# Expert inputs: nine gathers of quarter tokens replaced by three gathers of whole tokens, a store in slot order and four plain loads

## The chip, the core and the metric

The kernel runs as one program on one core of one Trainium2 chip. The metric is device time in microseconds (us), lower is better; the number quoted is the median of several runs, and one more execution was recorded by the hardware profiler. Where this text says PE, DVE, ACT, POOL and SP it means the engines TensorE, VectorE, ScalarE, GpSimd and SyncE.

## What is computed

Local plus pooled attention gives 2304 tokens of 512 numbers. Two mixture-of-experts layers follow. In the first, each token goes to one of 8 experts, and each expert takes exactly 288 tokens:

```python
order = np.argsort(-flat)                 # gate logits of all (token, expert) pairs
for idx in order:
    tok, e = (int(idx) // E, int(idx) % E)
    if assigned[tok] >= 0 or counts[e] >= cap:
        continue
    assigned[tok] = e
...
for e in range(E):
    mask = assigned == e
    h = np.maximum(x[mask] @ w1[e], 0.0)
    out[mask] = h @ w2[e]
```

The second layer is a soft mixture: 32 slots are weighted sums over all tokens, each slot passes through an expert's two layers, and each token takes a weighted sum of the slots.

## The kernel before, in words

**Stages.** Attention writes the tokens to device memory as `x_dram`, one row of 2 KB for each token (L261). The gating stage finds the assignment by bisection (rounds) and `dispatch` turns it into a table of token numbers: `idx` is 96 x 24, and column 3e + c holds the tokens of slots 96c to 96c + 95 of expert e. At the end of `gating` stands a branch (`tc.If`, L876) on a flag: a slow exact path that these inputs don't take. All engines pass that branch before the expert stage begins; the text calls the moment at which they go on the join.

**Expert stage.** `moe` (L1155) runs a loop over e from -2 to 8. Each round issues the steps of a list written out by hand (`START` for e up to 0, `PERIOD` for 1 to 6, `END` for 7 and 8), and that list alone fixes the order on each engine; engines wait for each other through semaphores. A step ("gather", 1) in round e works for expert e + 1. The steps that matter here:

- `gather(e)`, L1178: brings the 288 tokens of expert e into the tile `xs`, cut in quarters: partition 32a + t of block b holds quarter a (128 numbers, 512 B) of token 32b + t. That takes nine indirect DMAs on POOL's queue, each with 128 row numbers out of `idx4`, a table of 128 x 72 that `dispatch` works out from `idx` with three matmuls and three DVE operations (L808 to L817). Expert 0 is different: its tokens come by `first_gather` (L1147, three indirect DMAs of 96 whole tokens, still before the branch) and are transposed on PE (L1195).
- `x_t(e, dt)`, L1185: for e over 0, four times a 32 x 32 block transpose of `xs` on DVE (L1202), then the split in a high part on ACT (L1203) and a low part on DVE (L1204). The next expert's gather may write `xs` only when all four transposes of this one are done.
- `split` (weights in a high and a low part, L1209 and L1211), `hidden` (twelve matmuls for each of eight column blocks, L1224 to L1227), `relu`, `h_rows`, `logits2`, `soft`, `weighted` (18 matmuls, L1310), `slots` (L1323), `scatter` (three indirect DMAs on POOL, L1302).

**Weights.** `Stream` loads them on SP's queue in tiles of 1 MB. A load is issued when a slot comes free, in the order of the list `todo`, and SP waits in order: what stands behind a waiting load waits too. Slots are 8 tiles `a` (they hold second-layer weights of experts 4 to 7 until those are used), 9 tiles `b`, and near the end `xs`, `x0`, `x1`, `P`, `c0`.

## Time and profile before

| what | value |
|---|---|
| median of 3 runs | 460.2 us (459.11 to 460.39) |
| the profiled execution, its own time | 457.83 us |
| its span (first to last instruction) | 455.7 us |
| PE busy | 399.2 us, 88% of the span |
| DVE, ACT, POOL busy | 280.0, 204.3, 172.3 us |
| bytes moved by DMA | 111.54 MB, mean 245 GB/s |
| the gathers L1180 on POOL | 63 instructions, 66.7 us busy |

The busy share of an engine says little here, since the stages have different limits: the expert stage runs from 216 to 406 us, and what a change in it is worth is read from the waits of PE there. Times in rows are counted from the start of the span. The 2.1 us between the span and the execution's own time lie around the program.

### The profile page before, as it was taken

To read this page: it belongs to the slowest core of one execution; us is meant where nothing else is said; L and a number is where in the kernel's file an instruction comes from. 1 tells how busy PE (TensorE), PEld (TensorE's weight loads), DVE (VectorE), ACT (ScalarE), POOL (GpSimd) and SP (SyncE) were. 2 spreads that over 40 slices of the span, in tenths; PEclk is the share of its full clock that TensorE was granted. 3 is DMA by queue.
4 is the path that set the end of the run, shared out by engine and by line. 5 is a ranking of instruction groups with operands and counts; after the bars stand their busy time and mean duration, and the time that the engine had idled before them with its cause. 6 is when DMAs were issued, how large, how long until landed. Compare 5 with 4: busy or idle time off the path is not lost.

```text
span 455.7 us, 11232 instructions
## 1 busy us (share of the span) xinstructions
PE 399.2 (88%) x4386; PEld 297.8 (65%) x4386; DVE 280.0 (61%) x741; ACT 204.3 (45%) x554; POOL 172.3 (38%) x274
## 2 busy tenths in 40 slices
PE   5897988988979779995969999999999999579994
PEld 5675656655545547763868797979797977343694
DVE  6667849667583647873456676675867673414263
ACT  0555343353433427883445555645555554302241
POOL 7254353352343310002717474747466402212000
PEclk9799989999998798999699999999999999899997
DMA  8878999999999739901133566676748497959995
GB/s 218 211 212 227 275 250 296 280 239 306 257 265 272 305 94 399 424 22 55 44 109 134 199 236 229 235 259 217 263 168 311 131 378 285 420 192 355 410 378 233
DMA packets 33210, 111.54 MB, mean 245 GB/s; under 512 B 7328, under 2 KB 16928, under 8 KB 24352
## 3 DMA queue, kind: packets, MB, share of 16 engines
q1 hardware_dynamic: 28000, 100.43, 64.8%
q10 hardware_dynamic: 2176, 5.31, 5.0%
q0 software_dynamic: 2976, 5.02, 3.9%
q8 instruction: 37, 0.61, 0.5%
q14 instruction: 21, 0.17, 0.1%
HBM read 101.01 MB, written 9.73 MB: 243 GB/s over the span
## 4 chain that ended last, share of the span: by engine, by line
PE 27%; DVE 7%; ACT 6%; POOL 5%; issue 4%; DMA 3%; DVEq 0%; ACTq 0%; POOLq 0%
POOL xs L1180 5%; PE g L1310 4%; PE h L1421 3%; DMA xs<-x_dram,idx 3%; ACT bd L1295 3%; PE g L1323 2%; PE h L1224 2%; PE m L1443 2%; PE l L1443 2%; PE h L1225 2%; PE h L1227 2%; PE m L1257 2%; PE t L1224 1%; DVE xs L1202 1%; DVE wl L1211 1%
## 5 line engine op out<-in xcount | busy, mean ns | idle before, releaser
L1180 POOL DMA_INDIRECT xs<-x_dram,idx x63 | 66.7, 1059 | 53.6 <-DVE xs L1202 36.4
L1211 DVE TENSOR_TENSOR wl<-b,wh 128x512 fp32r<-128x512 f32 x64 | 42.9, 681 | 15.5 <-ACT wh L1209 14.9
L1209 ACT ACTIVATE wh<-b 128x512 fp32r<-128x512 f32 x64 | 39.1, 623 | 11.7 <-PE h L1225 6.8
L1224 PE MATMUL h<-x,wh 128*128 128x288 f32 x128 | 39.3, 328 | 4.2 <-ACT wh L1209 4.2
L1310 PE MATMUL g<-hb,bd 128*128 128x256 f32 x144 | 34.6, 396 | 6.8 <-ACT bd L1295 6.8
L1224 PE MATMUL t<-x,wh 128*128 128x288 f32 x128 | 36.7, 309 | 0.7 <-ACT wh L1209 0.7
L1302 POOL DMA_INDIRECT lg_rows<-lt,idx x24 | 22.3, 929 | 37.3 <-DVE lt L1284 30.6
L1225 PE MATMUL h<-x,wh 128*128 128x288 f32 x128 | 36.2, 304 | 0.0
L1310 PEld LDWEIGHTS g<-hb,bd 128*128 128x128 f32 x144 | 27.7, 197 | 12.5 <-ACT bd L1295 8.4
L1225 PE MATMUL t<-x,wh 128*128 128x288 f32 x128 | 35.1, 295 | 0.0
L1224 PEld LDWEIGHTS h<-x,wh 128*128 128x128 f32 x128 | 25.1, 196 | 13.4 <-ACT wh L1209 9.8
L144 POOL TENSOR_TENSOR e<-e,sm 128x256 f32<-128x256 f32 (+1 forms) x24 | 14.6, 608 | 46.9 <-DVE sm L143 35.9
L1242 DVE STREAM_TRANSPOSE hb<-hT 128x288 f32<-128x288 f32 x64 | 27.3, 456 | 0.1
L133 ACT ACTIVATE e<-sd,mx 128x144 f32<-128x144 f32 (+1 forms) x48 | 17.6, 371 | 19.0 <-DVE mx L124 18.0
L1203 ACT ACTIVATE x<-xs 128x288 fp32r<-128x288 f32 x28 | 12.4, 443 | 29.6 <-DVE xs L1202 29.4
L1224 PEld LDWEIGHTS t<-x,wh 128*128 128x128 f32 x128 | 24.1, 188 | 2.3 <-ACT wh L1209 1.7
L1225 PEld LDWEIGHTS h<-x,wh 128*128 128x128 f32 x128 | 25.2, 197 | 0.3
L1225 PEld LDWEIGHTS t<-x,wh 128*128 128x128 f32 x128 | 24.1, 188 | 0.2
L201 ACT ACTIVATE sc<-sc 128x228 f32<-128x228 f32 x24 | 9.3, 393 | 32.3 <-DVE sc L197 32.3
L91 DVE TENSOR_REDUCE kd<-kT 128x288 f32<-128x1152 f32 x16 | 21.5, 1346 | 3.6 <-DMA kT<-in_k_dram 3.6
L1204 DVE TENSOR_TENSOR x<-xs,x 128x288 fp32r<-128x288 f32 x28 | 12.8, 459 | 16.7 <-ACT x L1203 16.7
L1227 PE MATMUL h<-x,wl 128*128 128x288 f32 x128 | 22.7, 301 | 0.0
(289 smaller groups left out, 1014.1 us busy)
## 6 DMA issues: line engine op xcount, KB each, us to landing
b<-in_moe_w_dram SPq DMA_DIRECT2D x35, 1024.0 KB, 7.7
a<-in_moe_w_dram SPq DMA_DIRECT2D x16, 1024.0 KB, 10.4
a<-in_moe_w2t_dram SPq DMA_DIRECT2D x8, 1024.0 KB, 11.3
qT<-in_q_dram SPq DMA_DIRECT2D x8, 576.0 KB, 6.6
x_dram<-xu SPq DMA_DIRECT2D x8, 576.0 KB, 3.4
vn<-in_v_dram SPq DMA_DIRECT2D x8, 512.0 KB, 8.9
b<-in_moe_w_dram SPq DMA_DIRECT2D x7, 512.0 KB, 10.6
a<-in_moe_w_dram SPq DMA_DIRECT2D x6, 512.0 KB, 10.1
```

What stands on the lines that cost most here:

```text
L91: nc.vector.tensor_reduce(s["kd"][:, :, bi], s["kT"][:, :, bi, 3:3 + S].rearrange("p h (t r) -> p h t r", r=4), axis=AX.X, op=ALU.add)
L133: nc.scalar.activation(e[:n, h], p[:n, h], AF.Exp, bias=mx[:n, h:h + 1], scale=1.0 / 128, accum_out=sm[:n, h:h + 1])
L1180: nc.gpsimd.indirect_dma_start(out=xs[:, 128 * b:128 * b + 128], out_offset=None, in_=x_dram.rearrange("n (a d) -> (n a) d", a=4), in_offs ...
L1209: nc.scalar.activation(wh, w, AF.Copy)
L1211: nc.vector.tensor_sub(wl, w, wh.bitcast(F32))
L1224: nc.tensor.matmul(p, wh[:, dt], xh[:, dt], start=dt == 0, stop=False)
L1225: nc.tensor.matmul(p, wh[:, dt], xl[:, dt], start=False, stop=False)
L1227: nc.tensor.matmul(p, wl[:, dt], xh[:, dt], start=False, stop=dt == 3)
L1242: nc.vector.transpose(st["hb", e][:, :, ft], st.pop(("hr", e, ft)).rearrange("p (b t) -> p b t", t=32))
L1302: nc.gpsimd.indirect_dma_start(out=lg_rows[3 * e + c], out_offset=bass.IndirectOffsetOnAxis(ap=idx[:, 3 * e + c:3 * e + c + 1], axis=0), i ...
L1310: nc.tensor.matmul(p, bd[:, b].rearrange("t g s -> t (g s)"), hb[:, b].rearrange("t f r -> t (f r)"), start=b == 0, stop=b == NC - 1)
L1443: nc.tensor.matmul(p[32 * g:32 * g + 32], h2T[gp][:, ft, 32 * g:32 * g + 32], WS["a2", 4 * gp + g, h][:, ft], start=ft == 0, stop=ft == 7, ...
```

## The change

The table `idx4`, its constant `quarter` and the operations that made it are gone. For each expert from 1 on, three indirect DMAs of 96 whole tokens (2 KB each) bring the tokens into a new tile `xg`; one plain DMA on SP stores them as 288 consecutive rows of a new buffer `x_sorted` in device memory; four plain DMAs on SP, one for each quarter and 32 partitions each, load them from there into `xs` in the same layout as before, in pieces of 512 B. The work is spread: `gather(e)` loads expert e, stores e + 1 and gathers e + 2 (the first rounds fill this line). `xg` takes the room of the ninth `b` slot, and becomes a weight slot itself when the last expert has been stored.

```diff
-def gating(nc, tc, ctx, L, C, Z, idx, idx4, fill, first, force=None):
+def gating(nc, tc, ctx, L, C, Z, idx, fill, first, force=None):
...
             verdict(bad, what)
-
-        t96 = sb.tile([96, 24], F32, name="dt96", bufs=1)
-        nc.vector.tensor_copy(t96, idx)
         if what is not None:
             fill.run(psum, "t")
-        i4 = idx4.rearrange("p (c b) -> p c b", b=3)
-        for b in range(3):
-            sl = slice(32 * b, 32 * b + 32)
-            p = psum([128, 24])
-            nc.tensor.matmul(p, C["gsum"][sl], t96[sl], start=True, stop=True)
-            nc.vector.tensor_scalar(i4[:, :, b], p, 4.0, C["quarter"], op0=ALU.mult, op1=ALU.add)
...
     def gather(e):
-        for b in range(NC if e else 0):
+        if e == 0:
+            gather_rows(1)
+            return store_rows(1)
+
+        for a in range(4):
+            nc.sync.dma_start(xs[32 * a:32 * a + 32, 0:128 * NC].rearrange("p (b d) -> p b d", d=128),
+                              x_sorted[CAP * e:CAP * e + CAP, 128 * a:128 * a + 128].rearrange("(b t) d -> t b d", t=32))
+        if e == 1:
+            gather_rows(2)
+        if e + 1 < E:
+            store_rows(e + 1)
+        if e + 2 < E:
+            gather_rows(e + 2)
+        if e + 1 == E - 1:
+            WS.add_slots(mp, ["xg"])
+
+    def gather_rows(e):
+        st["xg"] = mp.tile([128, 2048], F32, name="xg", bufs=1)
+        for c in range(3):
             nc.gpsimd.indirect_dma_start(
-                out=xs[:, 128 * b:128 * b + 128], out_offset=None,
-                in_=x_dram.rearrange("n (a d) -> (n a) d", a=4),
-                in_offset=bass.IndirectOffsetOnAxis(ap=idx4[:, NC * e + b:NC * e + b + 1], axis=0))
+                out=st["xg"][0:96, DM * c:DM * c + DM], out_offset=None, in_=x_dram,
+                in_offset=bass.IndirectOffsetOnAxis(ap=idx[:, 3 * e + c:3 * e + c + 1], axis=0))
+
+    def store_rows(e):
+
+        nc.sync.dma_start(x_sorted[CAP * e:CAP * e + CAP].rearrange("(c w) d -> w c d", w=96),
+                          st["xg"][0:96, 0:3 * DM].rearrange("w (c d) -> w c d", c=3))
...
-        WS.add_slots(wb, [f"b{i}" for i in range(9)])
+        WS.add_slots(wb, [f"b{i}" for i in range(8)])
```

**POOL after the join.** The rows of POOL's program from the start of the expert stage on, before (`bd` is a tile of zeros, `lt` the rows that `scatter` writes; "x9" counts equal instructions):

```order
L1236 MEMSET bd_4095 128x1152
L1180 DMA xs_2606<-x_dram_72,idx4_2609 128x128 x18
L1302 DMA lg_rows<-lt_4404,idx_2608 2304x32 x3
L1180 DMA xs_2606<-x_dram_72,idx4_2609 128x128 x9
L1302 DMA lg_rows<-lt_4650,idx_2608 2304x32 x3
```

and of the change:

```order
L1246 MEMSET bd_4066 128x1152
L1186 DMA xg_4076<-x_dram_71,idx_2604 96x512 x3
L1186 DMA xg_4168<-x_dram_71,idx_2604 96x512 x3
L1186 DMA xg_4173<-x_dram_71,idx_2604 96x512 x3
L1186 DMA xg_4378<-x_dram_71,idx_2604 96x512 x3
L1312 DMA lg_rows<-lt_4384,idx_2604 2304x32 x3
```

Nine indirect DMAs for an expert become three, and before the first `scatter` the change gathers experts 1 to 4 where the kernel before gathered 1 and 2.

**SP after the join.** Before, SP's queue holds weight loads alone there:

```order
L919 DMA b1_4229<-in_moe_w2_dram 128x2048
L919 DMA b0_4284<-in_moe_w1_dram 128x2048
L919 DMA b2_4430<-in_moe_w1_dram 128x2048
L919 DMA b3_4501<-in_moe_w2_dram 128x2048
L919 DMA b4_4553<-in_moe_w2_dram 128x2048
L919 DMA b5_4559<-in_moe_w1_dram 128x2048
```

and of the change:

```order
L1192 DMA x_sorted_72<-xg_4076 96x3x512
L1172 DMA xs_2602<-x_sorted_72 32x9x128 x4
L1192 DMA x_sorted_72<-xg_4168 96x3x512
L907 DMA b1_4209<-in_moe_w2_dram 128x2048
L907 DMA b0_4264<-in_moe_w2_dram 128x2048
L1172 DMA xs_2602<-x_sorted_72 32x9x128 x4
L1192 DMA x_sorted_72<-xg_4173 96x3x512
L907 DMA b2_4410<-in_moe_w1_dram 128x2048
L907 DMA b3_4481<-in_moe_w1_dram 128x2048
L907 DMA b4_4533<-in_moe_w2_dram 128x2048
L907 DMA b5_4539<-in_moe_w2_dram 128x2048
```

In each period four loads and a store of tokens now stand in front of the four weight loads, and with one slot fewer the weight loads run one tile behind: the pair after the first store is both halves of expert 1's second layer, where before one of these was loaded ahead of the branch.

**PE ahead of the branch.** Before (L738 is the matmul of the flag, L530 and L514 are filler work for another tile, L816 makes `idx4`):

```order
L738 MATMUL g_3343<-bad,ones 1x2
L530 MATMUL t<-pt,gsum_70 32x128 x4
L816 MATMUL t<-dt_3347,gsum_70 128x24 x3
L514 MATMUL t<-wT,phi 32x256 x8
L530 MATMUL t<-pt,gsum_70 32x128 x4
L745 TENSOR_LOAD flag
L876 COMPARE_AND_BRANCH
```

and of the change:

```order
L735 MATMUL g_3336<-bad,ones 1x2
L529 MATMUL t<-pt,gsum_70 32x128 x4
L513 MATMUL t<-wT,phi 32x256 x8
L529 MATMUL t<-pt,gsum_70 32x128 x4
L742 TENSOR_LOAD flag
L864 COMPARE_AND_BRANCH
```

The three matmuls for `idx4` are gone from between the two pieces of filler work; nothing else moved on PE there.

## Rows read from the trace of the kernel before

**Rows 1.** Windows of the first expert and a later period: busy, PE clock, DMA share, GB/s.

```profile
212.00:234.00 22.00, 13.52 (x84) 12.88 (x77) 7.88 (x15) 6.78 (x14) 10.34 (x10) 0.77 0.13 39
254.00:275.00 21.00, 20.78 (x149) 17.53 (x150) 14.81 (x34) 11.86 (x29) 12.32 (x12) 1.00 0.66 231
```

**Rows 2.** Timeline of PE, the first matmuls of `weighted` in three periods: start, length.

```profile
295.68 1.56 PE L1310 MATMUL g<-hb,bd 128*128 128x256 f32 x6 [0.23 <-ACT bd L1295]
...
316.61 1.56 PE L1310 MATMUL g<-hb,bd 128*128 128x256 f32 x6 [0.22 <-ACT bd L1295]
...
338.00 1.35 PE L1310 MATMUL g<-hb,bd 128*128 128x256 f32 x5 [0.22 <-ACT bd L1295]
```

**Rows 3.** Timeline of DVE, first transpose for expert 1, 5 and 6; idle before in brackets.

```profile
231.14 0.48 DVE L1202 STREAM_TRANSPOSE xs<-xs 128x288 f32<-128x288 f32 x1 [2.94 <-DMA xs<-x_dram,idx]
...
317.08 0.48 DVE L1202 STREAM_TRANSPOSE xs<-xs 128x288 f32<-128x288 f32 x1 [2.36 <-issue]
...
337.71 0.48 DVE L1202 STREAM_TRANSPOSE xs<-xs 128x288 f32<-128x288 f32 x1 [1.60 <-DMA xs<-x_dram,idx]
```

**Rows 4.** Timeline of PE: its wait in the first expert, idle before in brackets.

```profile
233.48 0.40 PE L1224 MATMUL h<-x,wh 128*128 128x288 f32 x1 [3.14 <-ACT wh L1209]
```

**Rows 5.** Timeline of POOL after the join: first, second and last row of this stretch.

```profile
216.38 1.06 POOL L1236 MEMSET bd<- 128x1152 f32 x1 [4.92 <-DVEq L876]
217.59 0.97 POOL L1180 DMA_INDIRECT xs<-x_dram,idx  x1 [0.15 <-issue]
...
228.36 0.94 POOL L1180 DMA_INDIRECT xs<-x_dram,idx  x1 [0.30 <-issue]
```

**Rows 6.** Line L1150 (first_gather, three times 96 whole tokens): issue to landing.

```profile
DMA to landing us min/median/max: 3.0/3.0/3.0
```

**Rows 7.** Timeline of PE ahead of the branch.

```profile
209.67 0.53 PE L816 MATMUL t<-dt,gsum 32*128 32x24 f32 x6 [0.40 <-DVE dt L809]
210.13 1.07 PE L514 MATMUL t<-wT,phi 128*32 128x256 f32 x16
211.71 0.43 PE L530 MATMUL t<-pt,gsum 128*32 128x128 f32 x8 [0.51 <-ACT pt L518]
```

**Rows 8.** Timeline of ACT ahead of the branch.

```profile
207.69 2.06 ACT L501 ACTIVATE wT<-t 128x512 f32<-128x512 f32 x4 [1.06 <-PE t L499]
```

**Rows 9.** Line L876, the branch on PE's queue: duration in ns, start.

```profile
L876 PEldq COMPARE_BRANCH  x1: 3412/3412/3412, 212.3 to 212.3; - x1
```

**Rows 10.** DMA issues of the page: count, KB each, median us to landing.

```profile
b<-in_moe_w_dram SPq DMA_DIRECT2D x35, 1024.0 KB, 7.7
...
x_dram<-xu SPq DMA_DIRECT2D x8, 576.0 KB, 3.4
...
out_dram<-b SPq DMA_DIRECT2D x4, 576.0 KB, 3.0
```

**Rows 11.** Timeline of SP: a load of V (292.5 KB) into 32 partitions.

```profile
32.89 0.33 SPq L80 DMA_DIRECT2D V<-in_v_around_dram  x1
```

**Rows 12.** Window just behind that load: columns as in rows 1.

```profile
33.50:34.00 0.50, 0.50 (x7) 0.00 (x0) 0.50 (x2) 0.01 (x1) 0.00 (x0) 1.00 0.97 185
```

**Rows 13.** Timeline of SP: two weight loads at the end of a period.

```profile
302.98 1.19 SPq L919 DMA_DIRECT2D b<-in_moe_w_dram  x2
```

**Rows 14.** Windows behind those two loads.

```profile
309.00:310.00 1.00, 1.00 (x8) 0.89 (x7) 0.00 (x0) 0.39 (x2) 0.72 (x1) 1.00 1.08 438
...
311.00:312.00 1.00, 1.00 (x10) 1.00 (x10) 0.87 (x3) 0.97 (x4) 0.73 (x1) 1.00 0.21 66
```

**Rows 15.** Timeline of PE: its wait for the last expert.

```profile
396.31 1.22 PE L1310 MATMUL g<-hb,bd 128*128 128x256 f32 x2 [4.97 <-ACT bd L1295]
```

**Rows 16.** Windows in which the granted PE clock fell (first two) and rose (last).

```profile
214.50:215.00 0.50, 0.00 (x0) 0.00 (x0) 0.00 (x0) 0.00 (x0) 0.00 (x0) 0.91 0.00 0
...
395.50:396.00 0.50, 0.00 (x0) 0.00 (x0) 0.00 (x0) 0.49 (x2) 0.50 (x1) 0.81 0.97 410
399.00:399.50 0.50, 0.50 (x3) 0.44 (x2) 0.00 (x0) 0.00 (x0) 0.00 (x0) 0.77 0.28 79
```

More of the change, by code (lines that the diff above doesn't have):

```diff
@@ L460, in constants @@
     C["gsum"] = pool.tile([128, 128], F32, name="gsum4")
-    C["quarter"] = pool.tile([128, 1], F32, name="quarter")
     return C
@@ L598, in gate_consts @@
     C["pcol"] = pc
-    for g in range(4):
-        nc.gpsimd.memset(C["quarter"][32 * g:32 * g + 32], float(g))
     j = pool.tile([128, NT], F32, name="jrow")
@@ L1152, in first_gather, with moe @@
             in_offset=bass.IndirectOffsetOnAxis(ap=idx[:, c:c + 1], axis=0))
-def moe(nc, tc, ctx, C, WS, P, idx, idx4, mp, xs, x_dram, lg_dram, out):
+def moe(nc, tc, ctx, C, WS, P, idx, mp, xs, x_dram, x_sorted, lg_dram, out):
     ident, gsum = C["ident"], C["gsum"]
@@ L1509, in fused @@
     x_dram = dr.tile([N, DM], F32, name="x_dram")
+    x_sorted = dr.tile([N, DM], F32, name="x_sorted")
     lg_dram = nc.dram_tensor("lg_rows", [N, SL], F32, kind="Internal").ap()
@@ L1550, in fused @@
     idx = mp.tile([96, 24], I32, name="idx")
-    idx4 = mp.tile([128, 9 * E], I32, name="idx4")
     with ExitStack() as gctx:
-        WS.add_slots(wb, [f"b{i}" for i in range(9)])
+        WS.add_slots(wb, [f"b{i}" for i in range(8)])
         for e in range(4, E):
             PM.add(e)
-        gating(nc, tc, gctx, L, C, Z, idx, idx4, PM,
+        gating(nc, tc, gctx, L, C, Z, idx, PM,
                lambda: first_gather(nc, xs, x_dram, idx))
     pctx.close()
-    moe(nc, tc, ctx, C, WS, P, idx, idx4, mp, xs, x_dram, lg_dram, out)
+    moe(nc, tc, ctx, C, WS, P, idx, mp, xs, x_dram, x_sorted, lg_dram, out)
 _INS = ['q', 'k', 'v', 'v_rest', 'v_around', 'moe_w_gate', 'moe_w1', 'moe_w2', 'moe_w2t', 'moe2_phi', 'moe2_w1', 'moe2_w2']
```

## The prediction

> **What bounds the kernel now.** I read the windows by stage first, then the waits of PE, then what ended each. In a period of the expert stage PE is busy 20.78 of 21 us at full clock [rows 1], and the first matmuls of `weighted` follow each other after 20.93 us (295.68 to 316.61) and then 21.39 us (316.61 to 338.00) [rows 2]. So the periods are bound by PE, all but one: in the period with 21.39 DVE stood idle 2.36 us before the first transpose of the next tokens, which began at 317.08, 0.47 after `weighted` had begun [rows 2, 3]. In the neighbour DVE stood idle too (1.60 us), but its transpose at 337.71 came 0.29 ahead of `weighted`, and that period was not longer [rows 2, 3]. The reader is to see that a late gather is free until it pushes the transposes past `weighted`; the excess of 21.39 over 20.92 is then 0.47 us. The chain of waits runs through the gathers in every period all the same, since there they end just in time; a place on that chain is not a saving.
>
> The first expert is another case: in 212 to 234 PE is busy 13.52 of 22 us [rows 1]. All engines go on after the branch at 216.38 [rows 5]. Nine gathers for expert 1 start between 217.59 and 228.36 [rows 5], 1.35 apart, the last lands, and DVE, idle for 2.94, transposes at 231.14 [rows 3]. ACT and DVE hold the next weights' split behind that, so PE waits 3.14 us, from 230.34 to 233.48 [rows 4], 2.34 after the transpose began. PE can gain at most those 3.14 there.
>
> **The change part by part.**
>
> *The table `idx4`.* PE waited 0.40 us for the input of its three matmuls, which began at 209.67; the filler work behind them began at 210.13 [rows 7], 0.86 after PE was free (209.67 less 0.40 is 209.27). Without them it can begin at 209.27, since ACT has its first input ready halfway through four operations that run from 207.69 to 209.75, and the second at 209.75 [rows 8]. PE is the last to pass the branch: its compare takes 3.41 us from 212.3 [rows 9], and the join comes 0.6 behind its end. If those 3.41 us are a duration and not a date, the join moves from 216.38 to 215.53, by 0.85. Both ends: 0 (it waits on something that I don't see) and 0.85; I take 0.85, since nothing but PE's own rows stands ahead of it. The four DVE operations and the constant's four small memsets are on no chain that I found.
>
> *The first tokens, now through device memory.* From the join: POOL's memset and the first gather take 1.21 us as before (216.38 to 217.59), the third gather starts two spacings of 1.35 later [rows 5], at 219.44. The same shape (96 whole tokens) landed 3.0 us after its start [rows 6]: 222.44. Then SP stores 576 KB: 3.4 us for `x_dram`, in pieces of 512 B, and 3.0 for an output of the same size in long rows [rows 10]; pieces of 2 KB lie between, I take 3.2: 225.64. Then four loads of 144 KB in pieces of 512 B, each to 32 partitions. No such load is in the trace. The lower bound is the 3.4 of `x_dram` [rows 10], the same bytes and pieces on all partitions. A load to 32 partitions [rows 11] moved 185 GB/s with the DMA engines 0.97 busy [rows 12]; 576 KB at that rate are 3.15 us, where the 3.4 hold about 2.0 of data by my estimate (3.4 less some 1.4 for start and receipt: 0.6 from issue to the first bytes, rows 11 and 12, and as much again at the end), so 4.5 us in all. The upper bound adds three more issues of 0.33 [rows 11]: 5.5. I take 4.5, the nearest row's rate, and get 230.14. The transpose moves from 231.14 to 230.14: **1.0 us**, of which 0.85 is the join. The three transfers in a row take as long as the nine gathers did.
>
> The Trainium skill speaks against this part too: "SBUF — State Buffer", section "Door 1: The DMA port swizzle", says that 32 partitions reach half of the ports that DMA has, with a ceiling of about 218 GB/s, and that several transfers to different partitions don't add up to a full one. The 185 GB/s here agree; by its ceiling the four loads would take 0.5 us less and the whole change would save 0.5 more.
>
> *The later experts.* Rows are gathered two rounds ahead and stored one ahead, so only the four loads are left in the round itself. They stand on SP behind the two weight loads at a period's end (302.98 and the next, done by 304.17) [rows 13], whose bytes flow at 438 GB/s and have ended by 311 [rows 14]. The token loads come behind them in the same queue: 311 plus 3.15 and a receipt is 314.8 at the latest. DVE reaches the transposes at 314.72 (317.08 less 2.36 [rows 3]) and PE feels them past 316.6, so they arrive with nearly 2 us to spare. The 0.47 us of the one late period go: **0.47**. The other periods are bound by PE and give nothing.
>
> *What is added elsewhere.* SP: five more issues a period at some 0.35 us, on a queue that has four; what stands behind them are weight loads. POOL: six indirect DMAs fewer for an expert, and POOL is not waited for after that. DMA traffic: one store and one load of 576 KB, at most 3.15 us each by [rows 12], on 0.66 x 21 = 13.9 us of a period [rows 1]: 20.2 of 21 at the worst, so it still fits, without much room. Weights: with eight slots each load waits for one release more, but a half of expert e's first-layer weights is still loaded more than a period (20.9 us) before its use and lands in 7.7 [rows 10]. The sixth round's extra load (`xg` turned into a slot) falls where no rows are gathered any more, and from there on the number of slots is the old one, so the tail of the kernel is untouched. I cost all this at nothing; the cover is PE's 20.9 us a period, and if it were gone, each microsecond by which the tokens came too late would be paid six times.
>
> *Sum.* 1.0 + 0.47 = 1.47, against the profiled execution's own 457.83: 456.36. The median of the runs shown, 460.2, lies 2.4 above that execution; the same saving makes 458.7. About 0.3% (1.4 us) is what a measurement of this kernel can tell from no change, and the forecast stands just at that bound.
>
> **The rivals.**
>
> *The join stays and the chain is slower.* If PE's compare ends at the same date, or the loads take 5.5, one of the two terms of the first expert goes: 1.47 less 0.85 or less 1.0 leaves 0.5 to 0.6 of gain, 459.7. For it: I can't see what the 3.41 us wait for. Against it: the other engines passed the branch without such a wait, so it is PE's own. Same within the bound.
>
> *Slower: the PE clock falls in the longer wait.* The granted clock went to half (1.2 GHz) in windows where PE had done nothing since 212.14, 2.8 us earlier, and since 391.34, about 4.4 us earlier [rows 7, 15, 16]; a wait of 3.14 us did not bring it down [rows 4]. If the join stays and the store (3.4) and the loads (5.5) are slow, the transpose comes at 232.2, PE goes on 2.34 later, and its wait from 230.34 is 4.2 us. The half clock of the second case lasted 3.4 us (395.9 to 399.2) [rows 16], which costs half of that, 1.7. Then 1.05 later, 1.7 for the clock, less 0.47: 2.3 us slower, 462.5. It decides from a wait of PE of about 4 us on, that is a transpose later than 232.
>
> *Slower: the loads miss each period.* If token loads queue behind more weights than in [rows 13, 14], x comes 3 us later than I say, and 1 us over the slack in six periods costs 6: 466. Against it: 2 us of slack, and a DMA share of 0.66.
>
> *Faster by more.* With the store at 3.0 and the loads at 3.4 the transpose comes at 228.8: 2.3 + 0.47 = 2.8 saved, 457.4.
>
> **How the numbers follow.** Forecast 0.38 (457.8 to 459.2 by its own bounds, of which two thirds fall on the side of faster), faster by more 0.20, the join or the loads cancel it 0.25, the clock 0.10, loads late in each period 0.07. Faster by over 0.3%: 0.20 and 0.26 of the forecast, 0.46. Slower: 0.17. Same: 0.37. The predicted time is 458.7. The range reaches down past the faster case to 457.0 and up to the clock's 462.5; the loads late in each period and a little below lie outside.
>
> **What the profile after would show.** PE's compare at 211.4 instead of 212.3 and the join at 215.5; third gather 3.9 us after the join, the store landing at 225.6, the four loads at 230.1; PE's wait in the first expert of some 3 us, with the clock at full rate; no idle time of DVE ahead of the first transpose in later periods, and all `weighted` 20.9 apart; POOL's line of gathers at 21 instructions. Wrong would make it: a compare on PE that ends at 215.7 as before, token loads that land later than 316 in their period, a PE wait that ends on weights that came late, or an order of landing in which the store waits behind weight loads.

## The result and the profile after

The change took 464.11 us (median of 13 runs, 460.99 to 470.56) where the kernel before, timed beside it, took 461.84 (13 runs, 458.05 to 467.67): a ratio of 1.0105, with a 95% interval from 1.0067 to 1.0142. That ratio is taken from runs in the faster of the kernel's two states alone; the two medians stand at 1.0049. The change is slower, by 0.5 to 1%, against a forecast of 0.3% faster, and outside the range. The profiled execution took 461.2 us with a span of 459.5.

The timeline of the changed kernel, in order of time; the columns are start, length, engine, line, operation, and in brackets the idle time before and what ended it.

```profile
206.93 1.16 POOL L1138 DMA_INDIRECT xs<-x_dram,idx  x1 [4.02 <-DVE bad L730]
...
215.10 1.06 POOL L1246 MEMSET bd<- 128x1152 f32 x1 [4.56 <-PEq L864]
...
218.77 0.92 POOL L1186 DMA_INDIRECT xg<-x_dram,idx  x1 [0.30 <-issue]
...
222.78 0.34 SPq L1192 DMA_DIRECT2D x_sorted<-xg  x1
226.63 1.83 SPq L1172 DMA_DIRECT2D xs<-x_sorted  x4
...
231.98 0.48 DVE L1212 STREAM_TRANSPOSE xs<-xs 128x288 f32<-128x288 f32 x1 [4.50 <-DMA xs<-x_sorted]
...
234.33 0.40 PE L1234 MATMUL h<-x,wh 128*128 128x288 f32 x1 [4.73 <-ACT wh L1219]
...
255.52 4.12 PE L1320 MATMUL g<-hb,bd 128*128 128x256 f32 x18 [0.20 <-ACT bd L1305]
...
297.31 1.99 PE L1320 MATMUL g<-hb,bd 128*128 128x256 f32 x8 [0.22 <-ACT bd L1305]
...
316.27 0.43 DVE L1212 STREAM_TRANSPOSE xs<-xs 128x288 f32<-128x288 f32 x1
...
318.23 1.99 PE L1320 MATMUL g<-hb,bd 128*128 128x256 f32 x8 [0.22 <-ACT bd L1305]
...
339.15 2.21 PE L1320 MATMUL g<-hb,bd 128*128 128x256 f32 x9 [0.22 <-ACT bd L1305]
...
397.45 2.08 PE L1320 MATMUL g<-hb,bd 128*128 128x256 f32 x4 [4.97 <-ACT bd L1305]
```

The chain of expert 1 can be read off link by link. The third gather starts 3.67 us behind the join (215.10 to 218.77), SP issues the store 4.01 later, the first of the four loads 3.85 after that, and DVE transposes 5.35 after that: 16.88 us, where [rows 3, 5] have 14.76 (216.38 to 231.14). PE waits 4.73 us instead of 3.14 [rows 4]. Later it is as forecast: `weighted` at 297.31, 318.23 and 339.15 is 20.92 apart in both periods, where [rows 2] had 21.39 in the second, and DVE reaches the transpose at 316.27 with no idle time before it, where it stood idle 2.36 us in [rows 3].

The branch on PE's queue and the windows of the same kernel; the windows' columns are start:end, length, busy time of PE, PEld, DVE, ACT and POOL with instructions, PE's granted clock, the DMA share and GB/s.

```profile
L864 PEldq COMPARE_BRANCH  x1: 4266/4266/4266, 210.6 to 210.6; - x1
```

```profile
235.00:238.00 3.00, 3.00 (x15) 3.00 (x14) 1.42 (x5) 1.23 (x4) 0.28 (x1) 0.50 0.93 274
254.00:275.00 21.00, 20.80 (x151) 17.59 (x151) 14.70 (x34) 11.87 (x30) 4.85 (x5) 1.00 0.86 287
...
409.00:412.00 3.00, 2.67 (x16) 0.70 (x20) 0.55 (x3) 0.00 (x0) 1.76 (x7) 0.50 1.01 426
```

The compare starts earlier than in [rows 9] and lasts longer. The middle window stands beside [rows 1]: PE is as busy as before while the DMA share rises from 0.66 to 0.86. In the first and last window PE runs at half clock.

To see where the difference comes from I profiled the unchanged kernel a second time ("the second profile of before", run b0) and the change a second time (a2), on one chip, and measured all four from the first indirect gather for expert 0 on, which stands ahead of all that the change moves in the expert stage. That gather and `weighted` of expert 0 in the first profile of before:

```profile
207.85 1.17 POOL L1150 DMA_INDIRECT xs<-x_dram,idx  x1 [4.01 <-DVE bad L733]
...
253.88 4.12 PE L1310 MATMUL g<-hb,bd 128*128 128x256 f32 x18 [0.20 <-ACT bd L1295]
```

The stretches of the four profiles:

| us | before, first | before, second | change, first | change, second |
|---|---|---|---|---|
| first gather to POOL's memset at the join | 8.53 | 8.27 | 8.17 | 7.89 |
| join to first transpose of expert 1 | 14.76 | 14.26 | 16.88 | 17.03 |
| that to `weighted` of expert 0 | 22.74 | 23.47 | 23.54 | 23.72 |
| to `weighted` of expert 7 | 142.43 | 142.44 | 141.93 | 141.83 |
| sum, first gather to last `weighted` | 188.46 | 188.44 | 190.52 | 190.47 |
| from there to the end | 59.39 | 62.15 | 62.05 | 62.04 |

Between the first gather and the last `weighted` the change costs 2.06 and 2.03 us, 0.45% of the run: 2.6 more at the first expert, 0.5 to 0.6 given back, nearly all in the period that had been late. In the first pair the 2.6 are 2.12 of chain and 0.80 behind it, where PE ran at half clock in the change alone, less 0.36 of the join; in the second pair, where both ran at half clock there, they are 2.77 and 0.25 less 0.38. The last row is not the change's: the second profile of before has the same long tail, with the same stretch at half clock.

The timeline of the second profile of before, and its windows there.

```profile
209.01 1.17 POOL L1150 DMA_INDIRECT xs<-x_dram,idx  x1 [4.01 <-DVE bad L733]
...
217.28 1.06 POOL L1236 MEMSET bd<- 128x1152 f32 x1 [4.66 <-PEq L876]
...
231.54 0.48 DVE L1202 STREAM_TRANSPOSE xs<-xs 128x288 f32<-128x288 f32 x1 [2.96 <-DMA xs<-x_dram,idx]
...
233.88 0.40 PE L1224 MATMUL h<-x,wh 128*128 128x288 f32 x1 [3.05 <-ACT wh L1209]
...
255.01 4.12 PE L1310 MATMUL g<-hb,bd 128*128 128x256 f32 x18 [0.20 <-ACT bd L1295]
...
397.45 2.08 PE L1310 MATMUL g<-hb,bd 128*128 128x256 f32 x4 [4.97 <-ACT bd L1295]
```

```profile
235.00:238.00 3.00, 3.00 (x14) 3.00 (x13) 1.42 (x4) 1.86 (x5) 0.00 (x0) 0.50 0.71 232
409.00:412.00 3.00, 2.76 (x16) 0.80 (x20) 0.45 (x3) 0.00 (x0) 2.08 (x8) 0.50 1.01 426
```

In the first profile of before, the first of these windows is at full clock:

```profile
235.00:238.00 3.00, 2.48 (x19) 2.24 (x18) 1.96 (x4) 1.77 (x5) 0.00 (x0) 1.00 0.85 303
```

From 209.01 to 397.45 are the 188.44 of the table, and both half-clock windows are in the second profile without the change. Where the first gather itself starts says nothing of the change: at 207.85 and 209.01 before, at 206.93 and 206.69 with the change, and at 211.82 in another profile of the same changed kernel (a0, below).

### The profile page after: what moved, and what is told of

Its sections match the earlier page's. It is cut to its first block, busy times and chain, and to the rows that moved or that the text cites. A ratio compares the mean times of both kernels' runs of the same rounds, so it can differ in the third digit from the quotient of the medians.

```text
span 459.5 us, 11203 instructions
## 1 busy us (share of the span) xinstructions
PE 402.2 (88%) x4380; PEld 300.4 (65%) x4380; DVE 279.6 (61%) x737; ACT 204.2 (44%) x554; POOL 127.0 (28%) x228
## 4 chain that ended last, share of the span: by engine, by line
PE 34%; ACT 5%; DVE 5%; DMA 4%; issue 2%; POOL 1%; SPq 1%; DVEq 0%; ACTq 0%; POOLq 0%
PE g L1320 7%; PE h L1431 3%; ACT bd L1305 3%; PE g L1333 3%; DMA xs<-x_sorted 3%; PE h L1234 2%; PE t L1234 2%; PE m L1267 2%; PE t L1235 2%; PE h L1237 2%; PE h L1235 2%; PE t L1237 2%; PE m L1453 2%; PE l L1453 2%; DVE wl L1221 1%
## 5 line engine op out<-in xcount | busy, mean ns | idle before, releaser
L1312 POOL DMA_INDIRECT lg_rows<-lt,idx x24 | 23.5, 977 | 65.4 <-DVE lt L1294 59.3
L1186 POOL DMA_INDIRECT xg<-x_dram,idx x21 | 20.7, 986 | 72.9 <-DMA x_sorted<-xg 68.5
```

The costliest lines, as they stand in the source:

```text
L1186: nc.gpsimd.indirect_dma_start(out=st["xg"][0:96, DM * c:DM * c + DM], out_offset=None, in_=x_dram, in_offset=bass.IndirectOffsetOnAxis(ap ...
L1312: nc.gpsimd.indirect_dma_start(out=lg_rows[3 * e + c], out_offset=bass.IndirectOffsetOnAxis(ap=idx[:, 3 * e + c:3 * e + c + 1], axis=0), i ...
```

## The experiments

The theory after the result was "chain": what is lost is lost in the first expert, because three dependent transfers take longer there than nine gathers. The rivals were "traffic" (the store and load of 576 KB in each period slow the weights), "clock" (the half clock behind the longer wait is the loss) and "tail". The runs were made on several chips. On the chip of a2, b0, e10 and e11 the kernel before took 462.3 us (32 runs), as in the first comparison; in four other groups of runs, on three chips, it took 490 to 494; what their profiles show of it stands in the last section. There only medians of the changed kernel and of kernels built on it are compared with each other.

**One expert by the old way, one by the new (e1, e2, e3, e4).**

e1: the change, with `idx4` again and expert 1 by nine gathers.

```
-        if e == 0:
-            gather_rows(1)
-            return store_rows(1)
+        if e == 1:
+            ... nine indirect gathers of quarters, as before
-        for a in range(4):
+        for a in range(4 if e > 1 else 0):
```

> The changed kernel with expert 1 fetched as before the change (nine quarter gathers out of the table idx4, which is worked out again); experts 2 to 7 by gather, store and plain loads. If the loss comes from the first expert's longer chain (first-chain theory): PE's wait in the first expert is back at 3.1 to 3.2 us with its clock at full rate, the 0.47 of the one late period stays won, and the kernel takes 0 to 0.5 us less than before, ratio 0.997 to 1.003. If it comes from the added DMA traffic or the missing slot: still slower by about the 1% that the whole change costs, with PE waits on weights or on tokens in later periods.

e2: the kernel before, with expert 1 alone gathered whole, stored and loaded, and eight weight slots.

```
+        if e == 0: three gathers into xg; store to x_sorted
+        if e == 1: four loads from x_sorted; xg becomes a slot
-        for b in range(NC if e else 0):
+        for b in range(NC if e > 1 else 0):
```

> The kernel before with expert 1 alone fetched by three gathers of whole tokens, one store and four loads; experts 2 to 7 by nine quarter gathers, table idx4 kept, eight slots until expert 1 is stored and nine from there. First-chain theory: PE's wait in the first expert grows to 4.7 us or more (the table's 0.8 is not taken out ahead of the join, so 5.5 us at most), its clock falls in it, and the kernel is slower than before by at least the 1.6 us that this stretch lost in the profile of the change, ratio 1.004 to 1.012. Traffic theory: only one of seven experts has the extra bytes, so within 0.3% of before.

e3: the kernel before, with expert 1's gathers later by a memset.

```
     def gather(e):
+        if e == 1:
+            nc.gpsimd.memset(xs[:, 0:128 * NC], 0.0)
```

> The kernel before with one memset of 128 x 1152 zeros on POOL (1.06 us by the row of the same shape) ahead of the nine gathers of expert 1; nothing else differs, the zeros are overwritten. It makes expert 1 late without store, loads, traffic or a missing slot. First-chain theory: transposes 1.06 us later, PE's wait 4.2 us instead of 3.1, and if the clock falls in a wait of that length some 0.8 more: 1.0 to 2 us slower in the profile, ratio 1.002 to 1.010. If the loss belongs to the store, the loads or their traffic: 1.06 us of wait and no more, ratio at most 1.002.

e4: the kernel before with eight slots and, for five experts, four loads and one store of the change's sizes beside the nine gathers. The loaded rows are not used, and the stored ones are zeros.

```
+        if 2 <= e < E - 1:
+            ... four loads x_dram -> xg, one store of zeros -> x_sorted
```

> The kernel before with eight slots in place of nine and, for experts 2 to 6, four loads of 32 x 9 x 128 and a store of 96 x 3 x 512 on SP as the change has them, unconnected (rows of the token buffer into a tile that is not read, zeros into the sorted buffer). Traffic theory: slower by the 1% of the change. First-chain theory: within 0.3% of before, DMA share up by about 0.2 in the periods, gathers landing later but inside their slack except in the one late period, which may grow beyond its 0.47.

e1 took 467.21 us (6 runs), e2 495.56, e3 495.17, e4 495.36; the kernel before took 490.25 (11 runs, 480.67 to 501.77). The medians say little on the chain: e2, e3 and e4, with gathers of quarters, have `weighted` 24.4 to 28.5 us apart in the five periods that gather (20.1 and 17.3 in the last two, as everywhere), and the 2 us in question drown in that; e1 ran without the change beside it. What the profiles do show, on one chip, is the stretch from the join to the first transpose: 14.80 us in e1 and 14.90 in e4 with nine gathers, 17.45 in e3, where these start later, and 16.39 in e2 with gather, store and load. e2's store, loads and transpose:

```profile
223.59 0.34 SPq L1185 DMA_DIRECT2D x_sorted<-xg  x1
227.46 1.82 SPq L1189 DMA_DIRECT2D xs<-x_sorted  x4
...
232.78 0.48 DVE L1215 STREAM_TRANSPOSE xs<-xs 128x288 f32<-128x288 f32 x1 [4.72 <-DMA xs<-x_sorted]
```

I ran e1 again (as e1b) beside the change on another chip:

> The changed kernel itself, so that the three kernels beside it can be compared with it on one chip. On a chip like that of the first comparison: 461 to 467 us, ratio to before 1.005 to 1.014. On a chip like that of the four kernels before (before at 490 us, periods with nine gathers of 25 to 27.5 us): 20 to 27 us less than before.

> Expert 1 by nine quarter gathers with the table idx4, experts 2 to 7 as in the change; run again beside the change itself. First-chain theory: 2 to 5 us less than the changed kernel, if the gathers land as on the chip of the first comparison (wait of PE 3.1 to 3.2 us, clock at full rate). Traffic theory: within 0.3% of the changed kernel.

The change took 465.19 and e1b 467.14. e1b's transposes came 15.38 us after the join, where a0's came after 16.64, and its `weighted` of expert 0 came 1.0 sooner (48.71 after the first gather, a0 49.71), but its later periods took 1.06 more (143.34 to 142.28). The first expert fits the chain, but the 2 to 5 us that the theory expected were not gained, and what the later periods lost no run separates.

**The wait itself (e5, e6, e7).** e5 and e6 ran on the chip of a0, e7 on that of a1.

e5: the three gathers for expert 1 are issued ahead of the branch, right behind those of expert 0.

```
-    for c in range(3):
+    for e, t in enumerate((xs, xg1)):
+        for c in range(3):
...
-            gather_rows(1)
+            st["xg"] = xg1
```

> The change with the three gathers of expert 1 moved ahead of the branch, behind those of expert 0; POOL idles there for 4 to 5 us. Store and loads stay where they are. First-chain theory: the store goes right after the join, the loads land some 4 us earlier (transpose at 227.5 to 228 instead of 231.98), PE's wait of 4.73 us in the first expert shrinks to under 1 us, its clock stays at full rate there, and 4.5 to 6 us are gained on the changed kernel, 1 to 4 us on the kernel before. Traffic theory: the wait goes too, but the loss of the later stages stays: at most 4 us gained on the changed kernel.

463.75 us, 1.4 less than a0 with overlapping intervals, where 4.5 to 6 were expected. The wait for the chain is gone (join to transpose 11.79 us, first gather to `weighted` 2.7 less than a0), but the join comes 3 us later, and there filler work ahead of the branch waited on ACT while six gathers ran. PE's timeline, and the same place in the first profile of the change:

```profile
215.97 0.43 PE L529 MATMUL t<-pt,gsum 128*32 128x128 f32 x8 [3.63 <-ACT pt L517]
```

```profile
210.00 0.43 PE L529 MATMUL t<-pt,gsum 128*32 128x128 f32 x8 [0.48 <-ACT pt L517]
```

e6: ten matmuls, whose result is not read, fill PE's wait in the first expert.

```
     ("x_t", 1, 2),
+    ("busy", 0),
     ("hidden", 0, 7),
```

> The change with ten more matmuls of 128 x 288 on PE (some 4 us, result not read) in the place where PE waits 4.73 us for the weights behind expert 1's transposes. Nothing else moves. If the fall of the clock behind that wait is the wait's doing: no half clock between 230 and 245, x for expert 1 at the same time, 0.8 us gained in that stretch on the changed kernel, the tail as its own phase has it. If the fall comes by itself: the same stretch at half clock, 0 us gained, or up to 1 us lost if the matmuls run past the wait.

463.92 us, 1.3 less than a0 with overlapping intervals. The windows of e6, and of the unfilled change a0:

```profile
231.00:245.00 14.00, 13.48 (x84) 11.92 (x82) 7.12 (x15) 5.16 (x13) 4.83 (x5) 1.00 0.70 207
```

```profile
231.00:245.00 14.00, 9.14 (x57) 8.87 (x56) 6.03 (x12) 4.95 (x12) 3.96 (x5) 0.88 0.68 208
```

With PE kept busy the clock stays at 1.00 and the stretch from the transpose to `weighted` takes 22.70 us instead of 23.67 (a0) and 23.80 (a1). So the idle time brings the half clock here, and that costs 1.0 to 1.1 us, about as much as the two profiles of before differ by in that row of the table (22.74 and 23.47).

e7: the transposes of expert 1 stand later in `START`, behind more of expert 0's work.

```
-    ("x_t", 1, 0),   ahead of ("weighted", -1), and 1, 2, 3 behind it
+    ("x_t", 1, 0),   behind ("split", 0, 3)
+    ("x_t", 1, 2),   behind ("relu", 0, 1)
+    ("x_t", 1, 1),   behind ("hidden", 0, 3)
+    ("x_t", 1, 3),   behind ("h_rows", 0, 4)
```

> The changed kernel again, as the reference for the three beside it: 461 to 467 us, `weighted` of the first expert 40.3 to 40.4 us behind the join, 20.9 us apart from there.

> The change with one edit in the list START: the four x_t of expert 1 stand behind the last weight splits of expert 0, so that three more blocks of matmuls (4.8 us) are free to run while the tokens of expert 1 are on their way. First-chain theory: the wait of 4.73 us goes, PE waits at most 3 us behind that work instead, no half clock between 230 and 245, `weighted` of the first expert some 36.5 us behind the join instead of 40.4, and 2.5 to 4.5 us are gained on the changed kernel in the medians. If the loss is not the wait: less than 1 us gained.

463.85 us to a1's 463.67: nothing gained. The wait moved, as its timeline and window show:

```profile
246.22 1.17 PE L1267 MATMUL m<-hT,P 128*32 128x288 f32 x2 [4.52 <-ACT hT L1243]
```

```profile
243.00:252.00 9.00, 5.78 (x26) 3.90 (x27) 4.70 (x11) 3.45 (x8) 3.10 (x3) 0.62 0.97 291
```

PE now waits 4.52 us for ACT, whose relu stands behind the pieces of the transposes, and the clock falls there. First gather to `weighted` is 49.84, a1's 49.90, so the expectation failed and the edit decides nothing: the wait it was to remove came back in another place.

**Doses (e8, e9).** Both ran on the chip of a1. e8 adds two copies of 576 KB in pieces of 512 B, from device memory to device memory, for each expert; e9 puts a memset ahead of the three gathers for expert 1.

```
e8:
+            for r in range(2):
+                nc.sync.dma_start(x_extra[...]..., x_dram[...]...)
e9:
     def gather_rows(e, late=False):
+        if late:
+            nc.gpsimd.memset(st["xg"][:, 0:128 * NC], 0.0)
```

> The change with two more copies of 576 KB an expert from device memory to device memory in pieces of 512 B, as many bytes again as its store and loads; nothing waits for them except the queue. Traffic theory: the added 1.15 MB an expert costs again what the first cost, 2 to 5 us in the medians, with periods over 20.9 us. First-chain theory: periods stay at 20.9 us and the time within 0.4% of the changed kernel, unless the DMA share passes 1.0 in the periods (0.83 to 0.87 now, some 1.0 then) and weights come late.

> The change with one memset of 128 x 1152 (1.06 us) on POOL ahead of the three gathers of expert 1. First-chain theory: every microsecond by which that chain is later is paid in full, `weighted` of the first expert 41.4 to 41.5 us behind the join, the clock falls behind the wait as in the change, and the median is 1 to 2 us above the changed kernel. If the chain had slack: no change.

e8 took 532.31 us. Its window over six periods, and the same of the first profile of the change:

```profile
255.00:380.00 125.00, 89.25 (x574) 72.35 (x573) 57.36 (x129) 46.01 (x110) 23.67 (x24) 0.85 0.67 216
```

```profile
255.00:380.00 125.00, 123.14 (x879) 103.17 (x877) 87.41 (x202) 70.09 (x166) 29.77 (x31) 1.00 0.85 293
```

The share of DMA and the GB/s are lower in e8 than with the change, although the copies were added: the two copies of an expert write the same rows of `x_extra`, so SP issued the second only when the first had landed, and the weight loads stood behind both. One such pair on SP's queue:

```profile
259.52 17.52 SPq L1182 DMA_DIRECT2D x_extra<-x_dram  x2
```

Each of the two issues took 0.6 us by itself. So e8 measures a blocked queue and is no dose of the change's traffic. What speaks against "traffic" is the other row: with a share of 0.85 PE is busy 123.14 of 125 us in the change (123.10 before, in the same window), and the five periods in it take 20.87 to 20.92. e9 took 465.79, 2.1 more than a1 with overlapping intervals; its transposes came 0.51 later than a1's after the join (17.25 to 16.74), since the gathers themselves ran faster behind the memset: from the third gather to the store are 3.28 us, 3.80 in a1. Expected was `weighted` 41.4 to 41.5 us behind the join; it came 40.96 behind it (a1 40.54). The 0.51 was paid nearly in full, 0.42, but that profile is of e9's longest run (468.62), so it is weak evidence.

**The chain taken out (e10, e11, e12, e13).** In e10 expert 1 is handled like expert 0: PE transposes its gathered rows straight from `xg`, with no store and no load; expert 2 is gathered into `xs`, and all later experts stay as changed. In e10 to e13 expert 1's features stand in the order of expert 0's, but its weights in that of the later experts, so its part of the output is another; the amount of work is the same. e11 is e10 with twelve matmuls, whose result is not read, ahead of the last `weighted`. e12 and e13 are e10 and e11 with the gathers for expert 3 moved behind the transposes of expert 1.

```
e10:
-        if e == 0:
-            gather_rows(1)
-            return store_rows(1)
+        if e == 0:
+            return gather_rows(1)
-        for a in range(4):
+        for a in range(4 if e > 1 else 0):
...
-        if e == 0:
+        if e < 2:
+            rows = st["xg1"] if e else xs
e11, in weighted:
+        if e == E - 1:
+            for i in range(12):
+                nc.tensor.matmul(p, gsum, ..., start=True, stop=True)
e12, e13:
+            if (e, dt) == (1, 3):
+                gather_rows(3)
```

> The kernel before itself, profiled in a job of the later kind. If signals of PE come late while gathers run: periods of 24 to 27.5 us in place of 20.9, PE waiting for weight splits (wh) that had long been free to run, no waits on DMA, some 490 us. If the chip of the first comparison is met: 458 to 463 us and periods of 20.9.

> The changed kernel as the reference of the two beside it: 463 to 466 us, `weighted` of expert 0 about 40.0 us behind the first matmul after the join, 20.9 us apart from there, half clock behind the wait of 4.7 to 4.9 us in the first expert.

> The change with expert 1 handled as expert 0: its rows are transposed by twelve matmuls on PE (2.15 us by the row of expert 0) right out of the gathered tile, without store, loads and DVE transposes; the rows of expert 2 are gathered into the other tile meanwhile. First-chain theory: no wait of PE for expert 1 and no half clock behind it, `weighted` of expert 0 36.5 to 37.5 us behind the join in place of 40.0, and 2.5 to 3.5 us below the changed kernel in the medians. If the loss lies elsewhere: within 1 us of the changed kernel.

> The kernel of e10 with twelve more matmuls of 128 x 256 on PE (some 4.5 us, result not read) in the wait of 4.97 us ahead of the last expert's `weighted`. If the half clock from 395 on, and the one some 7 us behind it that comes in part of the runs, follow from that wait: no half clock between 390 and 420, `weighted` of the last expert 1 to 2 us shorter up to `slots`, and 1 to 3 us below e10 in the medians. If the clock falls there for another reason: no gain, up to 0.5 us lost.

| run | median us (runs) | ratio to before, 95% |
|---|---|---|
| b0, the unchanged kernel | 462.76 (10) | 0.9945 (0.9883 to 1.0007) |
| a2, the change | 462.90 (12) | 1.0057 (1.0014 to 1.0099) |
| e10 | 457.64 (12) | 0.9922 (0.9881 to 0.9963) |
| e11 | 455.97 (9) | 0.9893 (0.9846 to 0.994) |

With the chain gone the change loses 5.3 us of its median, more than the 2.5 to 3.5 expected. How far e10 is faster than before is less sure, since the unchanged kernel itself came out at 0.9945. The timeline of e10 with the first gather, PE at the place of [rows 4] and `weighted` of expert 0, and first and last of these in a2:

```profile
207.86 1.16 POOL L1138 DMA_INDIRECT xs<-x_dram,idx  x1 [4.01 <-DVE bad L730]
...
236.08 0.40 PE L1236 MATMUL t<-x,wh 128*128 128x288 f32 x1 [1.40 <-ACT wh L1221]
...
252.54 4.12 PE L1322 MATMUL g<-hb,bd 128*128 128x256 f32 x18 [0.20 <-ACT bd L1307]
```

```profile
206.69 1.16 POOL L1138 DMA_INDIRECT xs<-x_dram,idx  x1 [4.01 <-DVE bad L730]
...
255.33 4.12 PE L1320 MATMUL g<-hb,bd 128*128 128x256 f32 x18 [0.20 <-ACT bd L1305]
```

PE waits 1.40 us there, its clock stays at 1.00 from 230 to 245, and `weighted` of expert 0 comes 44.68 us after the first gather, 3.96 less than in a2 (48.64) and 1.32 less than in b0 (46.00); the later periods (141.91) stay as in a2. The rest of the 5.3, some 1.3 us, no stretch of the two profiles accounts for. The windows of e10 and of e11 around the last expert:

```profile
385.00:420.00 35.00, 27.04 (x184) 12.49 (x180) 12.16 (x32) 6.00 (x15) 7.33 (x19) 0.85 0.78 295
```

```profile
385.00:420.00 35.00, 31.26 (x232) 16.41 (x232) 12.26 (x33) 5.99 (x15) 7.91 (x20) 1.00 0.89 343
```

Filled, the wait for the last expert leaves the clock at 1.00, and from the last `weighted` to the end are 59.06 us instead of 61.85, as in the first profile of before (59.39).

> The kernel of e10 with the three gathers of expert 3 behind the transposes of expert 1 instead of ahead of them. First-chain theory: as e10, `weighted` of expert 0 some 36.4 us behind the join, no long wait of PE in the first expert, no half clock between 230 and 245, ratio to before 0.985 to 0.995 on a chip where before takes some 462 us (0.925 to 0.935 where it takes 490 to 494). If the time of e10 came from the wrong order: ratio 1.00 to 1.01 (0.94 to 0.95).

> The kernel of e12 with the twelve more matmuls (result not read) in the last expert's wait. If the clock's fall from 395 on follows from that wait: no half clock between 385 and 420, 1 to 3 us below e12 in the medians. Otherwise within 0.5 us of e12.

These two ran on a chip where the kernel before took 493.68 us: 462.25 and 462.23, ratios 0.9354 and 0.9352. `weighted` of expert 0 came 36.80 us behind the join in e12 (36.4 expected, 36.77 in e10), so moving the gathers for expert 3 changes nothing up to there. The medians gained nothing by the filler. The windows of e13 around the last wait and behind it:

```profile
395.00:405.00 10.00, 9.85 (x44) 8.20 (x44) 2.20 (x8) 2.63 (x8) 2.76 (x3) 1.00 0.91 373
405.00:412.00 7.00, 4.52 (x33) 1.75 (x36) 2.23 (x8) 0.00 (x0) 0.85 (x3) 0.90 0.58 208
```

Around the wait itself the filler keeps the clock at 1.00 here too, where e12 has 0.66; it falls later, behind 405, and from the last `weighted` to the end are 60.68 us instead of e12's 61.71. So filling the last wait is worth 2.8 us in one pair of profiles, 1.0 in the other and nothing in the medians of the second pair; e11's median is 1.7 below e10's with overlapping intervals.

## Why the prediction was wrong

*The first tokens, now through device memory*: this step failed, by the size of three of its terms. The third gather starts 3.67 us after the join (3.91 forecast); it hands over to the store after 4.01 (3.0, the landing alone, was taken), the store to the loads after 3.85 (3.2), the loads to the transpose after 5.35 (4.5). The sum is 16.88, in the second profile 17.03, where 14.61 was forecast and the gathers had taken 14.76. Each link took 0.65 to 1.0 us more than the row that it was priced from. For the gathers it is the landing itself; the line of `gather_rows` in this stretch, first profile of the change:

```profile
DMA to landing us min/median/max: 3.1/3.1/4.0
```

The like in [rows 6] was 3.0 for all three; one of 4.0 is enough, since the store waits for all. For the loads 1.83 of the 5.35 are the four issues, and the upper bound of 5.5 was nearly reached; how the rest divides between rate and receipt no run separates. The price left out that POOL gathers expert 2 beside these loads (227.26 to 230.72, DMA share 0.82 to 1.09 from 228 on); but in e2, which has no gather there and a weight load behind the four, the link took 5.32. The row it was priced from was also not as clean as I read it: the 185 GB/s of [rows 12] hold, beside the load to 32 partitions, one of 291 KB to 64 partitions that ACT's queue had issued just before:

```profile
32.74 0.50 ACTq L65 DMA_DIRECT2D kT<-in_k_dram  x1
```

So the 4.5 rested on no load of its kind alone, and 576 KB at 185 GB/s are 3.19 us, not 3.15. PE resumed 2.35 us after the transpose, 2.34 forecast, and its wait grew from 3.14 to 4.73. e10, which takes the store, the loads and DVE's transposes out for expert 1 alone and puts twelve matmuls on PE in their place, gets 3.96 back, the half clock behind the wait included.

*The table `idx4`*: 0.85 was forecast, and 0.36 and 0.38 came. The compare did begin sooner: 3.67 after the first gather (206.93 to 210.6) and 3.71 in the second profile, where the two profiles of before have 4.45 and 4.49. But it lasts 4266 and 3986 ns where it lasted 3412 and 3572. The rows of the second profiles, of before and of the change:

```profile
L876 PEldq COMPARE_BRANCH  x1: 3572/3572/3572, 213.5 to 213.5; - x1
```

```profile
L864 PEldq COMPARE_BRANCH  x1: 3986/3986/3986, 210.4 to 210.4; - x1
```

"If those 3.41 us are a duration and not a date" was the doubt that I named, and so was "it waits on something that I don't see". The trace's DMA records have something to see: in each of the twenty profiles one transfer of 16 KB on queue 8, of the kind that the profile's page calls "instruction", lies inside PE's compare, and the compare ends 1.32 to 1.38 us after that transfer has ended, however long it lasts.

| us | before, first | before, second | change, first | change, second |
|---|---|---|---|---|
| compare begins to transfer begins | 1.10 | 1.18 | 1.94 | 1.56 |
| the transfer | 0.99 | 1.04 | 0.96 | 1.06 |
| its end to the end of the compare | 1.32 | 1.35 | 1.36 | 1.36 |

So the length of the compare goes with a load of instructions, and with the change that load began later behind the start of the compare. Counted from the first gather the compare ends at 7.89 and 8.05 us before, at 7.95 and 7.67 with the change: the 0.78 were lost again, wholly in the first pair and half in the second. Why the load began later no run shows; in the twenty profiles it begins 1.00 to 1.95 us behind the compare's start. And "PE is the last to pass the branch" was not what [rows 5] say: there DVE's queue is named as what released POOL, 0.64 us after the compare had ended, where the other three profiles name PE's and have 0.22. So the 0.36 of the first pair owe nothing to PE, and the gain of the join is uncertain: two profiles of one kernel differ by 0.26 and 0.28 in it.

*The later experts*: right in mechanism and size. The five periods up to expert 5 are 20.87 to 20.92 (the last two are 20.1 and 17.3, as before), and the stretch of seven takes 141.93 and 141.83 instead of 142.43 and 142.44: 0.5 and 0.6, forecast 0.47.

*What is added elsewhere*: right at nothing. The DMA share is 0.85, PE stays at 20.80 of 21 us, and the rival of loads that miss each period did not come.

*The clock's rival* had the mechanism, and a wrong condition. The wait came to 4.73 and the clock fell behind it, but in the second profile of before it fell behind 3.05 too, and behind 3.14 in the first it did not; so "about 4 us" is no bound, and 0.7 to 1.1 us is its price, not 1.7. The chance of 0.10 that it got was too low: in the first pair of profiles its price came on top of the chain.

In sum the first expert cost 2.6 us instead of saving 1.0, the late period gave 0.5, and 2.05 remain: 0.45%. The ratios were 1.0105 and 1.0057 (the medians' own 1.0049 and 1.0013); the second one's interval holds 0.45%, the first one's does not. An identical kernel measured 0.9945 (0.9883 to 1.0007), so such a comparison can miss by half a per cent. Whether the change does more than the 2.05 outside the stretch measured, by more frequent half-clock stretches for instance, stays open: two profiles of each kernel don't tell.

## What to carry to other kernels

A gather that is replaced by gather, store and load is a chain of three hand-overs; price each from the start of one transfer to the issue of the next one that depends on it (here 4.0, 3.9 and 5.4 us), by the slowest of the transfers in it and with all issues, and keep the chain away from data whose first use is waited for; two rounds ahead of its use it cost nothing here. Profile the unchanged kernel twice and compare from a fixed instruction to a fixed instruction: a difference of 3.8 us between two spans was 2.05 of the change and the rest a clock and a start that vary by themselves. And a saving that a branch or a join lies behind is worth only what gets through it.

## What the runs showed of the hardware that was not expected

On three chips the kernel before took 490 to 494 us, 28 to 32 more than on the others. On two of them the change ran too, in 464 to 465, so that it is 5.5% faster there (0.9439, 0.9358 to 0.952, and 0.9454). The kernel before has no profile on those chips; the nearest is e3, which is that kernel and a memset. In it ACT takes up PE's results late while POOL's indirect DMAs run. The last matmuls of a tile and the relu behind them, first in the second profile of before, then in e3:

```profile
285.06 0.69 PE L1227 MATMUL h<-x,wl 128*128 128x288 f32 x4
...
285.85 0.41 ACT L1233 ACTIVATE hT<-h 128x288 f32<-128x288 f32 x1 [0.31 <-DVE hb L1242]
```

```profile
295.23 0.69 PE L1229 MATMUL h<-x,wl 128*128 128x288 f32 x4
...
296.75 0.41 ACT L1235 ACTIVATE hT<-h 128x288 f32<-128x288 f32 x1 [1.03 <-PE m L1259]
```

The matmuls end at 285.75 and 295.92; the relu follows 0.10 us later in the one and 0.83 in the other. The profile puts the wait in e3 down to the next matmuls (`m`, L1259), which end at 296.55; in the second profile of before the same relu began while those ran. Of the relus in e3 between 250 and 380 us that ACT was free to begin, all five start 0.79 to 0.85 us behind their matmuls, in the two profiles of before the like start 0.04 to 0.11 behind, and POOL's gathers run beside all of these. Without a gather at hand the lag in a0, on such a chip, is 0.09 to 0.21, and once 0.84, so the gathers are what it goes with and not a shown cause. The windows over six periods, of the first profile of before and of e3:

```profile
255.00:380.00 125.00, 123.10 (x877) 102.93 (x877) 87.68 (x202) 69.93 (x166) 64.11 (x63) 1.00 0.68 246
```

```profile
255.00:380.00 125.00, 107.93 (x740) 87.94 (x740) 74.55 (x170) 59.03 (x141) 63.02 (x59) 1.00 0.56 193
```

POOL is busy as long in both, and PE loses 15 of 125 us in the second, where the DMA engines have less to do. With three gathers for each expert POOL is busy 29.77 us (the change, above), and the seven periods of the change take 141.8 to 142.3 us in all four of its profiles (first, a0, a1, a2). Why some chips show it and others don't, the runs don't tell.
